# Moving bank-emptying copies and additions ahead of roundings, and the attention-row loads forward, at the start of a Strassen-style feed-forward

## The chip, the cores and the metric

The kernel runs on one core of a Trainium2 chip. The metric is device microseconds for one execution, as the median over runs. The other seven cores are not used.

## The reference, cut to what matters

Everything is float32; S = 2048 rows, D = 576 columns, H = 32 heads of 18, F = 4608.

```python
g = sigmoid((x * gate_w).sum(-1, keepdims=True))
# A: linear attention with a learned feature map (a pair of softmaxes per head)
phi_q, phi_k = softmax pairs of (q @ w_phi), (k @ w_phi)
a = (phi_q @ (phi_k^T v)) / (phi_q @ sum(phi_k) + 1e-6) @ wo
# B: gated ReLU feed-forward on the same x
b = (relu(x @ W_gate) * (x @ W_up)) @ W_down
out = g * a + (1 - g) * b
```

## The kernel before, in words

The kernel first computes the attention half (A) and writes its result, transposed and already scaled by the gate, to a DRAM tile `att` of 576 x 2048. Then it computes the feed-forward half (B), adding its results to rows of `att` that have been loaded back into SBUF, and writes the sums out.

All matrix products keep float32 accuracy by splitting each operand in a rounded high part and a low part ("high" is a copy on ScalarE into fp32r, "low" a subtraction on VectorE), and by multiplying high x high, high x low and low x high.

**The end of the attention half.** The 2048 columns are treated in four blocks of 512, in the order 3, 0, 1, 2 (`BLOCKS`), numbered b = 0 to 3. `project_out(b, m)` makes row block m of the output of block b: 14 matmuls for m < 4 and 9 for m = 4 into one PSUM bank, then `rows_out` copies the bank to SBUF on ScalarE (L796, or L798 and an addition on VectorE L799 for m = 4) and stores it to `att` (for b > 1 from GpSimd's queue). Its weights stand in four SBUF tiles of the pool `raw` (`WOUT`); the last projection, `project_out(3, 4)`, still reads three of them.

Between these last projections stands the preparation of the feed-forward. Seven sums of blocks of x, the operands of a seven-product (Strassen-Winograd) scheme, are numbered by their place in `SEQ = (1, 5, 6, 2, 7, 3, 4)`. Operands 3 to 6 are loaded in place: `high_in_place(0, i)` rounds one on ScalarE (L856, L857), `low_of_place(i)` makes its low part on VectorE (L861, L841), and `in_place(i)` does both. The weights of a unit are loaded to `wr` by `load_w`, rounded by `blocks`/`block_sums` with `high_w` (ScalarE L874), given low parts by `low_w` and `low_w_rows` (VectorE L877, L880), and their sums are formed by `sums_of_blocks` (VectorE L895 to L898). The results are `WB[u]` (tile `wb`) and `WS[u]` (tile `ws`), each in a pool of two buffers: those of unit u + 2 take the place of those of unit u. Because the second half of the rows needs the same weights again, the finished `wb` and `ws` are stored to DRAM (`wbd`, `wsd`), and a buffer is free for the next unit only when its store has landed.

**The units of the feed-forward.** There are 72 units u; each covers 128 columns of F for half of the rows. `step(u, j)`, j = 0 to 6, first issues one product of seven matmuls in the order of `SEQ`, then work on the other engines, then from the second pair of units on the down-projection of an earlier pair. The seven products use few banks, and accumulate on values that must first have been taken out:

- j = 0, product 1: a new bank `cx` (two in turn); j = 1, product 5: a new bank `ca` (one).
- j = 2, product 6: on top of `cx`, once `g1` has been copied from it (ScalarE L1299, issued at j = 1).
- j = 3, product 2: a new bank `cy`. j = 4, product 7: on top of `cx`, once `g2` has been copied (issued at j = 3).
- j = 5, product 3: on top of `ca`, once `u2` has been copied (issued at j = 2).
- j = 6, product 4: on top of `cx`, once `u2` has been added to it (VectorE L1420, issued at j = 5).

After that `g2` is added from `ca` (L1423) and gated (L1295), the last `cx` is gated at the next unit's j = 0, and the gated tiles are split (`hh` on ScalarE L1238, `hl` on VectorE L1243). Also in these steps: at j = 0 and 1 of unit u >= 1 the blocks of unit u + 1 are rounded and given low parts, at j = 2 their sums are formed, at j = 3 the sums are rounded, at j = 4 they get their low parts. At unit 0, j = 3 and 4, the down weights are rounded and given low parts (`plain_down`, L1096 and L1099).

**Order.** In this part the order on TensorE, VectorE, ScalarE, GpSimd and the SyncE queue (SP) is the order in which the code issues (`in_order`). So what stands behind a waiting instruction of the same engine waits too, and a DMA of SP behind one that waits. The attention rows of the first half are loaded by `load_acc` (L1141, eight times 256 KB) and `load_rest` (L1146, twice 128 KB) into `sums_of`, the four `raw` buffers that `WOUT` stood in.

Of the kernel before, what the change touches and what calls it, by code (L numbers as in the profile page):

```python
# [7 lines left out]
F32 = mybir.dt.float32  # L8
# [11 lines left out]
NC = F // P  # L20
# [63 lines left out]
def gated_mix_kernel(  # L84
# [717 lines left out]
    def project_out(b, m):  # L802

        i = 5 * (b - 1) + m + 1
        i = i % 2 if b < 3 else i % 4
        ps = pv1.tile([P, TB], F32, name="pw", tag="pv1") if i == 0 else kv_bank((2, 0, 1)[i - 1])
        accumulate(ps, [a for k in range(4, -1, -1) for a in pairs_of(b, m, k)])
        rows_out(b, m, ps)
# [135 lines left out]
    def in_place(i):  # L944
        high_in_place(0, i)
        low_of_place(i)

    def low_of_place(i):
        low_in_place(0, i)
        low_rest(0, i, tt)  # L950
# [48 lines left out]
    with in_order(tc, nc, nc.tensor, nc.vector, nc.scalar, nc.gpsimd, nc.sync):  # L999
        project_out(2, 1)  # L1000
        for k in (2, 1, 0):
            quotient(3, k)
        for k in (2, 1, 0):
            operand_rows(3, k)
        whole(x1)
        RS.close()
        pad = ctx.enter_context(tc.tile_pool(name="pad2", bufs=1, **R_))
        pad.tile([P, 24], F32, name="pad2")
        xo2 = ctx.enter_context(tc.tile_pool(name="xo2", bufs=4, **R_))
        wop = ctx.enter_context(tc.tile_pool(name="wop", bufs=2, **R_))  # L1010
        wraw = ctx.enter_context(tc.tile_pool(name="wraw", bufs=2, **R_))
        load_w(0)
        load_w(1)
        for i in range(3, 7):
            load_in_place(0, i)
        load_rests(0, (3, 4, 5))
        load_down(0)
        project_out(2, 2)
        blocks(0, high_w)
        low_parts(blocks, 0)  # L1020
        project_out(2, 3)
        project_out(2, 4)
        blocks(1, high_w)
        sums_of_blocks(0)
        operand_high(0, 2)
        project_out(3, 0)
        block_sums(0, high_w)
        low_parts(blocks, 1)
        operand_low(0, 2)
        load_rests(0, (6,))  # L1030
        load_w(2)
        low_parts(block_sums, 0)
        high_in_place(0, 3)
        project_out(3, 1)
        low_of_place(3)
        sums_of_blocks(1)
        high_in_place(0, 4)
        project_out(3, 2)
        block_sums(1, high_w)
        low_of_place(4)  # L1040
        high_in_place(0, 5)
        project_out(3, 3)
        low_parts(block_sums, 1)
        low_of_place(5)
        in_place(6)
        project_out(3, 4)
    AP.close()
    BS.close()
# [278 lines left out]
    def step(u, j):  # L1327


        g, odd = divmod(u, 2)  # L1330
        v, q = u + 1, g - 1
        plain, was_plain = g < NG or g == 2 * NG - 1, q < NG
        ps, first = bank(SEQ[j])
        product(ps, u, SEQ[j], first)
        add_up()
        make = 0 < u < NC - 1
        cx, ca, cy = (BANKS.get(n) for n in ("cx", "ca", "cy"))
        old = not odd and g > 0

        if j == 0:  # L1340
            if u > 0:
                last_cx, a = LATE.pop()
                gated(a, last_cx)
            if odd:
                EVEN[g] = LATE.pop(), a
            elif old:
                ODD[q] = EVEN.pop(q) + (LATE.pop(), a)
        e2, e1, o2, o1 = ODD[q] if old else EVEN[g] + (None, None) if odd else [None] * 4
        if odd and plain or old and was_plain:
            key, x2, x1 = ((g, 0), e2, e1) if odd else ((q, 1), o2, o1)  # L1350
            if j == 0:
                high_h(key + (1,), x2)
            elif j == 1:
                high_h(key + (0,), x1)
                low_h(key + (1,), x2)
            elif j == 2:
                low_h(key + (0,), x1)
        elif odd:
            if j == 1:
                high_h((g, 1), e1)  # L1360
            elif j == 3:
                low_h((g, 1), e1)
                minus(e2, e1)
            elif j == 4:
                high_h((g, 5), e1)
            elif j == 5:
                low_h((g, 5), e1)
        elif old:
            if j == 0:
                high_h((q, 6), e1)  # L1370
                minus(o2, e2)
            elif j == 1:
                high_h((q, 3), o2)
                low_h((q, 6), e1)
            elif j == 2:
                low_h((q, 3), o2)
                high_h((q, 7), e2)
                high_h((q, 2), o1)
            elif j == 3:
                minus(o1, e1)  # L1380
                low_h((q, 7), e2)
            elif j == 4:
                high_h((q, 4), e1)
                low_h((q, 2), o1)
            elif j == 5:
                low_h((q, 4), e1)

        if make:
            if j == 0:
                blocks(v, high_w)  # L1390
                if v + 1 < NC:
                    load_w(v + 1)
            elif j == 1:
                blocks(v, low_w)
                blocks(v, low_w_rows)
            elif j == 2:
                if v < NC - 2:
                    nc.sync.dma_start(wbd[v], WB.pop(v).bitcast(F32))
                sums_of_blocks(v)
            elif j == 4:  # L1400
                block_sums(v, low_w)
                block_sums(v, low_w_rows)
            elif j == 5:
                if v < NC - 2:
                    nc.sync.dma_start(wsd[v], WS.pop(v).bitcast(F32))
        elif j == 0 and NC < u < 2 * NC - 1:
            load_operands(v)

        if j == 1:
            T["g1"] = copy(cx, "g1")  # L1410
        elif j == 2:
            T["u2"] = copy(ca, "u2")
        elif j == 3:
            T["g2"] = copy(cx, "g2")
            if make:
                block_sums(v, high_w)
        elif j == 4:
            tt(out=T["g1"], in0=cy, in1=T["g1"], op=ADD)
        elif j == 5:
            tt(out=T["u2"], in0=cx, in1=T["u2"], op=ADD)  # L1420
        elif j == 6:
            a = T["g2"]
            tt(out=a, in0=ca, in1=a, op=ADD)  # L1423
            gated(a, T["u2"])
            if odd and not plain:
                minus(a, e1)
            LATE[:] = [a, (cx, T["g1"])]
            w = WO.pop(u)
            if NC - 2 <= u < NC:
                WO[u + 2] = w  # L1430

        if odd and plain and g > 0:
            if j == 2:
                plain_down(g, high)
            elif j == 3:
                plain_down(g, low)
        elif odd and not plain:
            prepare_down(g, 0, j)
        elif old and not was_plain:
            prepare_down(q, 1, j)  # L1440
        if old and j == 5:
            load_down(g)
        if old and j == 6:
            ODD.pop(q)
        if g > 0:
            s = 7 * odd + j
            PEND.append(down_plain(q, s) if was_plain else down(q, s, one_bank))

        swap_in(u, j)
        if u == 0:  # L1450
            if 3 <= j < 5:
                plain_down(0, (high, low)[j - 3])
            elif j == 5:
                nc.sync.dma_start(wbd[u], WB.pop(u).bitcast(F32))
                nc.sync.dma_start(wsd[u], WS.pop(u).bitcast(F32))
        if u == 1 and j < 2:
            (nc.sync.dma_start(wbd[u], WB.pop(u).bitcast(F32)) if j == 0 else
             nc.sync.dma_start(wsd[u], WS.pop(u).bitcast(F32)))
        if u == 1 and j == 6:
            for i in range(8):  # L1460
                load_acc(0, i // 2 % 2, i // 4, i % 2)
            load_rest(0)
        if u in (NC + 1, 2 * NC - 1) and j < 4:
            if j % 2 == 0:
                rest_copy(j // 2)
            else:
                rest_rows(u // NC - (u == NC + 1), j // 2)
        if u == NC + 1:
            if j == 6:
                store_rest(0, 0)  # L1470
                store_rest(0, 1)
                load_rest(1)
        if j == 6 and u < NC:
            if u >= 4:
                next(later_half, None)
            if u == NC - 3:
                for _ in later_half:
                    pass
                load_operand(1, 0)
                load_operand(1, 1)  # L1480
# [157 lines left out]
```

## Time and profile before

| what | value |
|---|---|
| median of 3 runs | 1583.54 us (1583.13 to 1584.26) |
| the profiled execution | 1582.98 us |
| its span | 1581.2 us (1.8 us lie around it) |
| TensorE busy | 1567.2 us, 99% |
| VectorE busy | 1189.2 us, 75% |
| ScalarE busy | 558.6 us, 35% |
| granted TensorE clock | 1.000 |
| DMA | 283.38 MB, mean 179 GB/s |

Times in the trace are microseconds from the start of the span. A row of the timeline gives the start, the duration, the engine, the line and operation, output<-input, how many instructions were merged, and in square brackets how long the engine had been idle before it and what ended that. Rows of an engine may overlap slightly, since the next instruction starts before the last one has drained. Unit 0 of the feed-forward begins at 338.30 us, unit 2 at about 364 us; the rest of the span is the other 70 units and the end.

### The profile page before, as it was taken

Reading aid. Unit: us, or ns where it says so; the run is one execution under the profiler, and the core shown is the slowest. Engines: PE = TensorE matmul, PEld = TensorE weight load, DVE = VectorE, ACT = ScalarE, POOL = GpSimd, SP = SyncE. Lnnn points to the kernel's source line nnn. Section 1 sums busy time; section 2 is a strip of 40 time slices with the busy share of each in tenths; the row PEclk is TensorE's granted clock in tenths of the full one; section 3 lists DMA queues with packets and bytes.
Section 4 is the critical chain, followed back from the end, with each engine's and each line's share of the span. In section 5 each row is a group of like instructions: output and inputs, shape, how many; then the busy total and the mean of one; then the engine's idle time right before and its main releaser. Section 6 shows DMA issues by size and latency. Waiting matters only on the chain.

```text
span 1581.2 us, 20182 instructions
## 1 busy us (share of the span) xinstructions
PE 1567.2 (99%) x7823; PEld 1311.4 (83%) x7823; DVE 1189.2 (75%) x1865; ACT 558.6 (35%) x918; POOL 175.1 (11%) x243
## 2 busy tenths in 40 slices
PE   9999999999999999999999999999999999999998
PEld 9999995677888888888888888888888888888887
DVE  4997775597787877887777777777767777777777
ACT  4344335563333333333333334232232322232321
POOL 0126521110000000000000002111111111111110
PEclk9999999999999999999999999999999999999999
DMA  5365315597755575556545516543443443543432
GB/s 172 108 214 185 146 50 158 168 350 253 256 201 212 212 278 204 201 212 224 196 172 206 220 44 236 191 183 132 153 183 132 162 160 131 178 159 132 185 136 75
DMA packets 64539, 283.38 MB, mean 179 GB/s; under 512 B 6802, under 2 KB 17298, under 8 KB 55740
## 3 DMA queue, kind: packets, MB, share of 16 engines
q1 hardware_dynamic: 61228, 270.34, 47.1%
q0 software_dynamic: 2352, 10.11, 1.9%
q10 hardware_dynamic: 864, 1.65, 0.3%
q8 instruction: 61, 1.00, 0.3%
q14 instruction: 34, 0.28, 0.1%
HBM read 172.07 MB, written 108.60 MB: 178 GB/s over the span
## 4 chain that ended last, share of the span: by engine, by line
PE 95%; DVE 3%; ACT 1%; DMA 0%; issue 0%; POOL 0%; SPq 0%; ACTq 0%; POOLq 0%
PE cx L1133 28%; PE ca L1133 14%; PE pd L1173 12%; PE pd L1196 10%; PE cy L1133 7%; PE kv L175 4%; PE pk L175 3%; PE pq L175 3%; PE pm L1173 2%; PE pm L1196 2%; PE kv L421 1%; PE po L562 1%; PE pv L237 1%; PE ptr L379 1%; PE pw L175 1%; PE psf L259 1%
## 5 line engine op out<-in xcount | busy, mean ns | idle before, releaser
L1238 ACT ACTIVATE hh<-g 128x512 fp32r<-128x512 f32 x195 | 120.0, 624 | 457.3 <-DVE g L1295 287.9
L1211 DVE TENSOR_TENSOR ac<-pd,ac 128x512 f32<-128x512 f32 x238 | 163.9, 689 | 144.4 <-PE pd L1196 144.2
L1133 PE MATMUL cx<-xo,ws 128*128 128x512 f32 x1008 | 252.0, 389 | 1.6 <-ACT g L1299 1.6
L1133 PE MATMUL ca<-xo,ws 128*128 128x512 f32 x1008 | 251.9, 389 | 0.0
L1133 PE MATMUL cx<-xo,wb 128*128 128x512 f32 x1008 | 249.0, 389 | 1.5 <-DVE u L1420 1.5
L1133 PEld LDWEIGHTS cx<-xo,ws 128*128 128x128 f32 x1008 | 189.2, 188 | 41.2 <-ACT g L1299 2.1
L1133 PEld LDWEIGHTS cx<-xo,wb 128*128 128x128 f32 x1008 | 188.2, 188 | 42.4 <-DVE u L1420 1.9
L1133 PEld LDWEIGHTS ca<-xo,ws 128*128 128x128 f32 x1008 | 189.2, 188 | 39.3
L1173 PE MATMUL pd<-hh,wd 128*128 128x512 f32 x576 | 200.7, 389 | 0.0
L1196 PE MATMUL pd<-hh,wd 128*128 128x512 f32 x476 | 185.2, 389 | 0.0
L1179 DVE TENSOR_TENSOR ac<-pd,ac 128x512 f32<-128x512 f32 x144 | 99.0, 688 | 105.6 <-PE pd L1173 102.8
L1243 DVE TENSOR_TENSOR hl<-g,hh 128x512 fp32r<-128x512 f32 x195 | 135.4, 694 | 1.9 <-ACT hh L1238 0.2
L1299 ACT ACTIVATE g<-cx 128x512 f32<-128x512 f32 x144 | 85.0, 590 | 129.2 <-PE cx L1133 129.1
L1173 PEld LDWEIGHTS pd<-hh,wd 128*128 128x128 f32 x576 | 108.1, 188 | 22.5
L1133 PE MATMUL cy<-xo,wb 128*128 128x512 f32 x504 | 125.9, 389 | 0.0
L1096 ACT ACTIVATE wd<-wdr 128x384 fp32r<-128x384 f32 (+1 forms) x106 | 62.3, 606 | 143.2 <-DMA wdr<-wd 143.2
L1173 PE MATMUL pd<-hl,wd 128*128 128x512 f32 x288 | 112.0, 389 | 0.0
L1133 PEld LDWEIGHTS cy<-xo,wb 128*128 128x128 f32 x504 | 94.6, 188 | 19.6
L1196 PEld LDWEIGHTS pd<-hh,wd 128*128 128x128 f32 x476 | 89.4, 188 | 18.5
L1196 PE MATMUL pd<-hl,wd 128*128 128x512 f32 x238 | 92.6, 389 | 0.0
L841 POOL TENSOR_TENSOR xo<-xr,xo 32x512 fp32r<-32x512 f32 x5 | 8.3, 1670 | 614.7 <-PE ca L1133 608.5
L874 ACT ACTIVATE ws<-wr 128x1536 fp32r<-128x1536 f32 x36 | 53.7, 1491 | 48.2 <-DVE wr L898 46.0
(256 smaller groups left out, 2572.1 us busy)
## 6 DMA issues: line engine op xcount, KB each, us to landing
wsd<-ws SPq DMA_DIRECT2D x34, 1280.0 KB
ws<-wsd SPq DMA_DIRECT2D x34, 1280.0 KB
wbd<-wb SPq DMA_DIRECT2D x34, 960.0 KB
wb<-wbd SPq DMA_DIRECT2D x34, 960.0 KB
wr<-wgu SPq DMA_DIRECT2D x36, 768.0 KB
wdr<-wd SPq DMA_DIRECT2D x36, 576.0 KB
eT<-et SPq DMA_DIRECT2D x10, 594.0 KB
xt<-xb SPq DMA_DIRECT2D x7, 768.0 KB
```

The lines of the kernel that those rows point to most:

```text
L175: nc.tensor.matmul(ps, w, m, start=i == 0, stop=i == len(pairs) - 1)
L237: nc.tensor.matmul(pv[i][c], m, w_[:, k, cs], start=k == 0 and n == 0, stop=k == 4 and n == 1)
L874: nc.scalar.activation(o[:, :, 0:3], a, AF.Copy)
L1096: nc.scalar.activation(o[:, 0], a, AF.Copy)
L1133: nc.tensor.matmul(ps, w, v, start=first and m == 0, stop=m == len(pairs) - 1, skip_group_check=True)
L1173: nc.tensor.matmul(ps, w, v, start=k == 0 and (i < 2 or first), stop=k == len(mms) - 1 and (i < 2 or last), skip_group_check=True)
L1179: tt(out=a, in0=ps, in1=a, op=ADD)
L1196: mm = lambda ps, w, v, a, z: nc.tensor.matmul(ps, w, v, start=a, stop=z, skip_group_check=True)
L1211: tt(out=a, in0=ps, in1=a, op=ADD)
L1238: nc.scalar.activation(h, src, AF.Copy)
L1243: tt(out=l, in0=src, in1=h.bitcast(F32), op=SUB)
L1299: nc.scalar.activation(a, ps, AF.Copy)
```

## The change

Three things change.

1. Among the last projections, the rounding of operand 5 (`high_in_place(0, 5)`) goes ahead of `project_out(3, 3)`, `block_sums(1, high_w)` goes behind it, and `in_place(6)` goes from ahead of `project_out(3, 4)` to unit 0, j = 1, behind the copy of `g1`.
2. In unit 1 the low parts of the block sums of unit 2 (`low_w`, `low_w_rows`) go from j = 4, ahead of the additions to `g1` and `u2`, to j = 5, behind them; the store of `ws` of unit 2 follows them as before.
3. The ten loads of attention rows go from the end of unit 1 to j = 0 of unit 0. On SP they now stand ahead of the stores of `wb` and `ws` of units 0 and 1 and of `load_w(3)`.

```diff
         high_in_place(0, 4)
         project_out(3, 2)
+        high_in_place(0, 5)
+        low_of_place(4)
+        project_out(3, 3)
         block_sums(1, high_w)
-        low_of_place(4)
-        high_in_place(0, 5)
-        project_out(3, 3)
         low_parts(block_sums, 1)
         low_of_place(5)
-        in_place(6)
         project_out(3, 4)
...
             elif j == 4:
-                block_sums(v, low_w)
-                block_sums(v, low_w_rows)
+                if u > 1:
+                    block_sums(v, low_w)
+                    block_sums(v, low_w_rows)
             elif j == 5:
-                if v < NC - 2:
+                if 2 < v < NC - 2:
                     nc.sync.dma_start(wsd[v], WS.pop(v).bitcast(F32))
...
         elif j == 5:
             tt(out=T["u2"], in0=cx, in1=T["u2"], op=ADD)
+            if u == 1:
+                block_sums(v, low_w)
+                block_sums(v, low_w_rows)
+                nc.sync.dma_start(wsd[v], WS.pop(v).bitcast(F32))
...
         if u == 0:
+            if j == 0:
+                for i in range(8):
+                    load_acc(0, i // 2 % 2, i // 4, i % 2)
+                load_rest(0)
+            elif j == 1:
+                in_place(6)
             if 3 <= j < 5:
                 plain_down(0, (high, low)[j - 3])
...
-        if u == 1 and j == 6:
-            for i in range(8):
-                load_acc(0, i // 2 % 2, i // 4, i % 2)
-            load_rest(0)
```

## The prediction

> **What bounds the kernel now.** The page comes first: it says which engine has no time to spare.
>
> ```profile
> span 1581.2 us, 20182 instructions
> PE 1567.2 (99%) x7823; PEld 1311.4 (83%) x7823; DVE 1189.2 (75%) x1865; ACT 558.6 (35%) x918; POOL 175.1 (11%) x243
> ```
>
> TensorE works for 1567.2 of 1581.2 us, so the change can only gain what TensorE stands idle. Next the waits of TensorE, longest first: only two of them lie where the change is made.
>
> ```profile
> PE cx L1133 <- ACT g L1299: 1.6, 1, 1.6
> PE cx L1133 <- DVE u L1420: 1.5, 1, 1.5
> ```
>
> Each occurred once. The timeline of TensorE shows where, and what each costs.
>
> ```profile
> 338.30 1.75 PE L1133 MATMUL cx<-xo,wb 128*128 128x512 f32 x7
> 339.89 1.75 PE L1133 MATMUL ca<-xo,ws 128*128 128x512 f32 x7
> ...
> 343.28 1.89 PE L1133 MATMUL cx<-xo,ws 128*128 128x512 f32 x7 [1.64 <-ACT g L1299]
> ...
> 359.28 1.75 PE L1133 MATMUL ca<-xo,ws 128*128 128x512 f32 x7
> 362.53 3.49 PE L1133 MATMUL cx<-xo,wb 128*128 128x512 f32 x14 [1.50 <-DVE u L1420]
> ```
>
> A product of seven matmuls occupies 339.89 - 338.30 = 1.59 us. Product 6 of unit 0 was therefore due at 341.48 and began at 343.28: 1.80 us lost, and its seven matmuls lasted 1.89 instead of 1.75, the matmuls right after a gap being slower: 0.14 more. Product 4 of unit 1 was due at 360.87 and began at 362.53: 1.66, and I take the same 0.14 for it. Together 1.94 + 1.80 = 3.74 us, 0.24% of the time. That is the most that the change can gain. 0.2% (3.17 us) is about what a measurement of this kernel can tell from no change, so the answer hangs on what is left of these 3.74.
>
> **The first stall.** ScalarE's timeline shows why the copy of `g1` came late:
>
> ```profile
> 337.08 1.49 ACT L874 ACTIVATE ws<-wr 128x1536 fp32r<-128x1536 f32 x1 [3.14 <-DVE wr L898]
> 338.48 1.04 ACT L856 ACTIVATE xo<-xo 128x1024 fp32r<-128x1024 f32 x1
> ...
> 339.94 0.58 ACT L796 ACTIVATE o<-kv 128x512 f32<-128x512 f32 x1
> 340.42 1.04 ACT L856 ACTIVATE xo<-xo 128x1024 fp32r<-128x1024 f32 x1
> ...
> 342.01 0.59 ACT L798 ACTIVATE o<-kv 64x512 f32<-64x512 f32 x1
> 342.63 0.60 ACT L1299 ACTIVATE g<-cx 128x512 f32<-128x512 f32 x1
> ```
>
> ScalarE idled 3.14 us for VectorE's sums, then ran the rounding of `ws`, operand 5, a bank copy, operand 6 and another bank copy, and only then `g1`, ready since 338.30 + 1.75 = 340.05. After the change operand 5 (338.48 to 339.94, 1.5 us) goes into the 3.14 us of idle time, which has room for it and for the bank copy (0.6) behind it. `ws` still starts at 337.08, the last bank copy follows at 338.5, and ScalarE is free at 339.1. `g1` is then copied at 340.1 to 340.7, before product 6 is due at 341.48. Operand 6 follows until 342.1; it delays `u2` to 342.7 and `g2`, whose product ends at 343.2, not at all. The first stall goes.
>
> **What is late next in unit 0: VectorE.**
>
> ```profile
> 336.97 1.22 DVE L861 TENSOR_TENSOR xo<-xo 128x1024 fp32r<-128x1024 f32 x1
> ...
> 342.85 1.23 DVE L861 TENSOR_TENSOR xo<-xo 128x1024 fp32r<-128x1024 f32 x1
> ...
> 344.82 0.68 DVE L799 TENSOR_TENSOR o<-o,kv 64x512 f32<-64x512 f32 x1
> 346.86 0.69 DVE L1418 TENSOR_TENSOR g<-cy,g 128x512 f32<-128x512 f32 x1 [1.36 <-PE cy L1133]
> 347.47 1.42 DVE L1099 TENSOR_TENSOR wd<-wdr,wd 128x1024 fp32r<-128x1024 f32 x2
> 348.80 0.68 DVE L1420 TENSOR_TENSOR u<-cx,u 128x512 f32<-128x512 f32 x1
> ```
>
> From 336.97 VectorE has no gap until L799 has run; the same work stands there after the change, in another order, so it is done at 344.82 + 0.71 = 345.53. Then come the addition to `g1`, the low part of the down weights and the addition to `u2`, which before followed each other at 0.61 and 1.33 us: 345.53, 346.14, 347.47, done at 348.15. Product 4 of unit 0 is due at 341.48 + 4 x 1.59 = 347.83. It waits for `u2` until 348.19: a new stall of 0.36 + 0.14 = 0.50 us. Before, TensorE's delay of 1.94 us covered this. Of the first stall 1.94 - 0.50 = 1.44 us are gained.
>
> **The second stall.** Low parts stood ahead of the additions:
>
> ```profile
> 357.72 1.49 ACT L874 ACTIVATE ws<-wr 128x1536 fp32r<-128x1536 f32 x1 [0.81 <-DVE wr L898]
> ...
> 359.24 1.22 DVE L877 TENSOR_TENSOR ws<-wr,ws 128x1024 fp32r<-128x1024 f32 x1 [1.61 <-ACT ws L874]
> 360.48 0.68 DVE L880 TENSOR_TENSOR ws<-wr,ws 32x512 fp32r<-32x512 f32 x1
> 361.19 0.69 DVE L1418 TENSOR_TENSOR g<-cy,g 128x512 f32<-128x512 f32 x1
> 361.80 0.68 DVE L1420 TENSOR_TENSOR u<-cx,u 128x512 f32<-128x512 f32 x1
> ```
>
> VectorE waited for ScalarE's rounding and then spent 361.19 - 359.24 = 1.95 us on L877 and L880 before it came to `g1` and `u2`. Moved behind `u2`, they no longer stand before product 4. Unit 1 begins at 348.19 + 1.59 + 0.14 = 349.92, its product 7 begins at 356.27 and ends at 358.0; `u2` is then added by 358.7, product 4 is due at 349.92 + 6 x 1.59 = 359.46. The stall goes, 1.80 us. The price: the low parts now stand before the addition of `g2` from `ca` and its gating. They end at 358.7 + 1.95 = 360.6, `g2` is out of `ca` at 361.3 and gated at 362.0 (0.7 us each, as the rows of L1418 and L1420); product 5 of unit 2 wants `ca` at 359.46 + 2 x 1.59 = 362.64. Cover 1.3 us; without it, up to 1.95 us would come back. What waits behind on ScalarE is the rounding of the gated tile, then `wb` of unit 3, then unit 2's `g1`, at about 364.9; before product 6 of unit 2 one down product (six matmuls, 1.36) is inserted, so it is due at 365.6. Cost nothing.
>
> **The loads on SP.** Here the queues change most.
>
> ```profile
> 332.78 0.33 SPq L870 DMA_DIRECT2D wr<-wgu  x1
> 333.16 0.43 SPq L1454 DMA_DIRECT2D wbd<-wb  x1
> ...
> 361.64 5.70 SPq L1141 DMA_DIRECT2D ac<-att  x8
> ```
>
> Before, the store of `wb` of unit 0 was issued at 333.16, and that of `ws` behind it. After, the ten loads stand ahead of them, and these wait for the `raw` buffers of the projection weights. One comes free as `project_out(3, 3)` ends, the others in the course of `project_out(3, 4)`: its nine matmuls of 1.59 / 7 = 0.23 us end just behind 338.30, so they began at 336.3, and with the 0.1 to 0.2 that a matmul takes to end the buffers come free between 336.4 and 338.5. So the stores come some ten us later, and ScalarE's rounding of `wb` of unit 2 may write only when the store of `wb` of unit 0 has landed:
>
> ```profile
> 351.95 1.15 ACT L874 ACTIVATE wb<-wr 128x1152 fp32r<-128x1152 f32 x1
> L1238 ACT ACTIVATE hh<-g 128x512 fp32r<-128x512 f32 x195 | 120.0, 624 | 457.3 <-DVE g L1295 287.9
> ```
>
> Behind it on ScalarE stand one `hh` (0.62) and unit 1's copy of `g1` (0.60). That copy is wanted by product 6 of unit 1, at 349.92 + 2 x 1.59 = 353.10. So the rounding must begin by 353.10 - 1.15 - 0.62 - 0.60 = 350.7; otherwise it can begin at 350.1, when product 4 of unit 0 is done with the buffer. When does the store land? The rates, from the windows; the last column is GB/s:
>
> ```profile
> 338.00:340.00 2.00, 2.00 (x11) 1.65 (x10) 1.94 (x3) 2.00 (x4) 0.00 (x0) 1.00 1.02 429
> ...
> 362.00:364.00 2.00, 1.47 (x6) 1.24 (x7) 1.77 (x3) 0.16 (x1) 0.00 (x0) 1.00 0.99 410
> 364.00:366.00 2.00, 2.00 (x10) 1.64 (x9) 1.54 (x3) 2.00 (x3) 0.00 (x0) 1.00 1.09 252
> 366.00:368.00 2.00, 2.00 (x11) 1.65 (x10) 1.18 (x2) 1.01 (x3) 0.00 (x0) 1.00 0.82 267
> 368.00:370.00 2.00, 2.00 (x11) 1.65 (x10) 0.16 (x1) 0.25 (x1) 0.00 (x0) 1.00 1.06 335
> 370.00:372.00 2.00, 2.00 (x11) 1.65 (x10) 1.97 (x4) 0.60 (x1) 0.00 (x0) 1.00 1.03 385
> ...
> 369.84 0.69 DVE L1179 TENSOR_TENSOR ac<-pd,ac 128x512 f32<-128x512 f32 x1 [2.65 <-DMA ac<-att]
> ```
>
> The store of a `ws` (1.31 MB) and the ten loads (2.36 MB) shared 362 to 372 us, the loads at 267 to 385 GB/s once the store was through: 6.1 to 8.8 us for the ten. By 368.0 some 2 x (0.410 + 0.252 + 0.267) = 1.86 MB had moved, the `ws` and two loads; the addition that needs the second load began at 369.84: 1.8 us from data moved to landed. After the change I let the loads' data move from 338.0, between the first and the last release (`load_w(2)`, issued at 332.78, goes first), with one `att` store among them (0.26 MB, 0.6 us): until 344.7 to 347.4. The `wb` store, 0.98 MB at 429 GB/s, takes 2.3 and 1.8 to land: 348.8 to 351.5, the middle 350.2. So its cost lies between nothing and 351.5 - 350.7 + 0.14 = 0.9 us. I take nothing, as the middle lies before 350.7. What follows on SP has more room. By the same rate `ws` of unit 0 lands 3.1 us behind it, at 353.3, and is wanted when `ws` of unit 2 is rounded, at 357.72 before and up to 1.9 earlier now; `load_w(3)` (0.79 MB) and `wb` of unit 1 land at 355.1 and 357.4 and are wanted at about 362.5, in unit 2's first step; `ws` of unit 1 lands at 360.5 and is wanted some steps later. The store of `ws` of unit 2, moved behind the additions, is wanted only two units on.
>
> The Trainium skill, "DMA: Bandwidth & Descriptors", section "Bandwidth", speaks against loads of this size: its table gives 138 GB/s at 64 KB and 341 at 1 MB and asks for 1 MiB per DMA; at some 250 GB/s for 256 KB, an estimate from that table, the ten would last 9.4 us, the store would land at about 352.1, and the gain would shrink to about 1.7 us. This trace agrees only in the first windows (252 and 267 GB/s); the later ones reach 385, as the loads queue up behind each other.
>
> VectorE's wait of 2.65 us for the loads in unit 2 (that last row) goes as well. That gains nothing, as TensorE waits for nothing there.
>
> **Sum.** 1.44 + 1.80 = 3.24 us. The profiled execution took 1582.98 us, 1.78 around its span, 0.56 below the median of the runs. It should become 1579.7 with a span of 1578.0, and the median 1583.54 - 3.24 = 1580.3.
>
> **The rivals.**
>
> *The store of `wb` is late (0.18).* For it: the loads' slow first windows, and transfers that were spread over 30 us now stand in one queue. Against: the middle of the estimate. A store landing between 350.7 and 352.5 takes 0.2 to 1.9 us back: 1580.5 to 1582.2, within 0.2%.
>
> *VectorE gets to `u2` in time (0.14).* If its chain is 0.4 us shorter than I add it up, the new stall in unit 0 vanishes and the gain is the whole 3.74: 1579.8. Against it: VectorE is packed without a gap from 336.97, and nothing of its work is taken away.
>
> *Slower (0.06): the loads wait for the last attention row.* `att` is one DRAM tile. If the loads are held until all of it is stored, not only the rows of blocks 0 and 1 that they read, they wait for the store behind L799:
>
> ```profile
> DMA to landing us min/median/max: 4.7/6.5/8.9
> ```
>
> L799 would end at 343.5, its store be issued at 344.1 and land, at the median of 6.5, at 350.6. From first issue to the landing of `wb` my estimate above takes 350.2 - 336.4 = 13.8 us, some 1.6 of it waiting for `load_w(2)`: the store lands at 362.8, and ScalarE is 12 us late for 350.7. That is 12 - 3.2 = 9 us slower, 1592.5. The tipping point is a landing at 350.7 + 3.2 = 353.9. Against it: the rows read are written by the projections of b = 1 and 2, well before. Such a stall would also be the only one here long enough for the clock. By the Trainium skill, "TensorE: Matmul & The Clock Gate", section "What's actually happening", an idle window of some 3.4 us halves the clock until a busy one has passed, which would add an estimated 1.7 us; no run here shows it.
>
> **How the numbers follow.** My forecast has 0.62. Its 3.24 us lie just above 3.17, and its terms are good to some 0.3 us, so I put 0.40 of it above 0.2% and 0.22 within. With the 0.14 of the full gain that makes faster 0.54, with the 0.18 of the late store same 0.40; slower is the last rival, 0.06. The forecast and the full gain, with runs that scatter by half a microsecond, reach from 1579.2; the late store reaches to 1582.2. The range 1579.2 to 1582.4 leaves out the slower case and the edges.
>
> **What would show it.** Right: TensorE's waits for `g` L1299 and for `u` L1420 at unit 1 are gone; a wait of some 0.4 us for `u` L1420 stands at about 348 us; unit 2 starts at about 361.1 instead of 364.3; SP issues the loads at 336 to 342 us; no wait of ScalarE for a DMA before `wb`. Wrong: an ACT `wb` L874 that idles for `wbd` at 350 to 352 us and a TensorE wait for `g` behind it, loads issued only after 350 us, or a stall in unit 2 for `g2` or `hh`.

## The result, and the profile after

| | median | lowest to highest | runs |
|---|---|---|---|
| before | 1583.60 us | 1582.97 to 1585.32 | 20 |
| after | 1581.57 us | 1580.04 to 1584.27 | 20 |

The ratio is 0.9986 [0.9980, 0.9992], 0.14% faster, and the medians lie 2.0 us apart. That is clear of the noise, but within the 0.2% that the prediction calls no change. The runs of after scatter over 4.2 us where those of before scatter over 2.4. The ratios here and below leave out the one slow run of all, 1736.76 us at a mean granted clock of 0.851, in experiment 8. The profiled execution of after happens to be the longest of its twenty, with 1584.27 us and a span of 1581.7, so its span shows no gain at all; the shortest span of the twenty is 1578.1, next to the 1578.0 that was forecast. Part of what separates them is seen below.

The page, and TensorE's waits (waiting instruction, releaser: us in total, times, longest), of the profiled execution of after:

```profile
span 1581.7 us, 20179 instructions
PE 1568.9 (99%) x7823; PEld 1312.1 (83%) x7823; DVE 1189.8 (75%) x1865; ACT 558.3 (35%) x918; POOL 175.2 (11%) x243
...
PE cx L1132 <- ACT g L1298: 1.9, 1, 1.9
```

Lines moved by one: the product's line 1133 is 1132 now, the copies' 1299 is 1298. Of the two old waits the one for VectorE's `u` is gone from the list. A wait for the copy `g` is still there, once and a little longer, but TensorE's timeline shows that it is another one:

```profile
338.33 1.75 PE L1132 MATMUL cx<-xo,wb 128*128 128x512 f32 x7
...
341.50 1.75 PE L1132 MATMUL cx<-xo,ws 128*128 128x512 f32 x7
...
346.26 1.75 PE L1132 MATMUL ca<-xo,ws 128*128 128x512 f32 x7
348.12 3.48 PE L1132 MATMUL cx<-xo,wb 128*128 128x512 f32 x14
...
355.07 2.54 PE L1132 MATMUL cx<-xo,ws 128*128 128x512 f32 x7 [1.89 <-ACT g L1298]
357.41 2.75 PE L1132 MATMUL cy<-xo,wb 128*128 128x512 f32 x7
360.00 1.75 PE L1132 MATMUL cx<-xo,ws 128*128 128x512 f32 x7
...
363.17 3.33 PE L1132 MATMUL cx<-xo,wb 128*128 128x512 f32 x14
```

Product 6 of unit 0 starts at 341.50, 3.17 us behind product 1, with no wait: the first stall is gone. Product 4 of unit 1 (363.17, the first half of 14 matmuls) starts with no wait: the second is gone too. The new stall is at product 6 of unit 1: 1.89 us idle, and then two products that take 2.54 and 2.75 us instead of 1.75. Why it waited, ScalarE's timeline tells:

```profile
340.11 0.60 ACT L1298 ACTIVATE g<-cx 128x512 f32<-128x512 f32 x1 [0.89 <-PE cx L1132]
...
349.50 0.63 ACT L1237 ACTIVATE hh<-g 128x512 fp32r<-128x512 f32 x1 [4.47 <-DVE g L1294]
352.85 1.16 ACT L874 ACTIVATE wb<-wr 128x1152 fp32r<-128x1152 f32 x1 [2.72 <-DMA wbd<-wb]
353.92 0.61 ACT L1237 ACTIVATE hh<-g 128x512 fp32r<-128x512 f32 x1
354.44 0.58 ACT L1298 ACTIVATE g<-cx 128x512 f32<-128x512 f32 x1
```

The rounding of `wb` of unit 2 could have started at 350.13 and waited 2.72 us until the store of `wb` of unit 0 had landed. The copy of `g1` stands behind it, two instructions on, and so started at 354.44. The SP queue and the windows show the store's way (last three columns of a window: granted clock, DMA share, GB/s):

```profile
336.48 4.61 SPq L1140 DMA_DIRECT2D ac<-att  x8
341.56 1.23 SPq L1145 DMA_DIRECT2D ac<-att  x2
343.16 0.45 SPq L1464 DMA_DIRECT2D wbd<-wb  x1
...
336.00:338.00 2.00, 2.00 (x10) 1.65 (x10) 1.97 (x3) 1.47 (x2) 0.46 (x1) 1.00 0.72 267
338.00:340.00 2.00, 2.00 (x11) 1.65 (x10) 1.94 (x3) 1.20 (x2) 0.07 (x1) 1.00 0.67 136
340.00:342.00 2.00, 2.00 (x11) 1.65 (x10) 1.95 (x3) 1.89 (x3) 0.00 (x0) 1.00 0.91 291
342.00:344.00 2.00, 2.00 (x11) 1.65 (x10) 1.94 (x4) 1.38 (x4) 0.04 (x1) 1.00 1.05 306
344.00:346.00 2.00, 2.00 (x10) 1.69 (x9) 1.94 (x3) 1.03 (x2) 0.52 (x1) 1.00 0.98 327
```

The ten loads are issued from 336.48, as forecast, and the store behind them at 343.16. While the loads are issued and run, 136 to 327 GB/s move. The store lands 9.7 us after its issue.

The two long products behind the gap are the clock. In the windows of one us the granted clock is 0.55, 0.50, 0.50 and 0.74 between 356 and 360, and 1.00 around that:

```profile
356.00:357.00 1.00, 1.00 (x5) 0.75 (x4) 0.97 (x3) 0.00 (x0) 0.00 (x0) 0.55 1.04 437
357.00:358.00 1.00, 1.00 (x4) 0.81 (x3) 0.93 (x3) 0.35 (x1) 0.00 (x0) 0.50 0.99 417
358.00:359.00 1.00, 1.00 (x4) 0.81 (x3) 0.54 (x1) 0.62 (x2) 0.00 (x0) 0.50 1.08 456
359.00:360.00 1.00, 1.00 (x5) 0.73 (x5) 0.00 (x0) 1.00 (x1) 0.00 (x0) 0.74 0.98 415
```

### The profile page after: what moved, and what is told of

It is laid out like the page before. It is cut to its first block, busy times and chain, and to the rows that moved or that the text cites. A ratio compares the mean times of both kernels' runs of the same rounds, so it can differ in the third digit from the quotient of the medians.

```text
span 1581.7 us, 20179 instructions
## 1 busy us (share of the span) xinstructions
PE 1568.9 (99%) x7823; PEld 1312.1 (83%) x7823; DVE 1189.8 (75%) x1865; ACT 558.3 (35%) x918; POOL 175.2 (11%) x243
## 3 DMA queue, kind: packets, MB, share of 16 engines
q10 hardware_dynamic: 864, 1.65, 0.3%
## 4 chain that ended last, share of the span: by engine, by line
PE 95%; DVE 2%; DMA 1%; ACT 0%; issue 0%; POOL 0%; SPq 0%; DVEq 0%; ACTq 0%; POOLq 0%
PE cx L1132 28%; PE ca L1132 14%; PE pd L1172 12%; PE pd L1195 10%; PE cy L1132 7%; PE kv L175 4%; PE pk L175 3%; PE pq L175 3%; PE pm L1172 2%; PE pm L1195 2%; PE kv L421 1%; PE po L562 1%; PE pv L237 1%; PE ptr L379 1%; PE pw L175 1%; PE psf L259 1%
```

## The experiments

**The measure.** The start of unit 0 itself lies between 338.3 and 341.5 us in the profiled executions of all kernels, two executions of after among them with 338.33 and 341.47: the attention half before it scatters by some 3 us, and this blurs totals. So beside the ratios I use the distance from product 1 of unit 0 to product 1 of unit 3 in TensorE's timeline. The places of unit 0 to 2 that the change touches lie within it. Most kernels, before among them, have one profiled execution and so one distance; the one kernel that was profiled twice without a late store repeats it to the hundredth (40.79). A stall found there costs more than the idle time listed: the idle time counts from the end of the last matmul, 0.16 us after the next one was due, and the product behind a gap takes 0.14 more. So a listed wait w costs w + 0.30, which gives the prediction's 1.94 and 1.80 for 1.64 and 1.50.

| kernel | unit 0 | unit 3 | distance | against before |
|---|---|---|---|---|
| before | 338.30 | 382.64 | 44.34 | |
| after, first profile | 338.33 | 383.12 | 44.79 | +0.45 |
| after, three more | 341.47, 338.32, 339.00 | 383.19, 380.63, 381.15 | 41.72, 42.31, 42.15 | -2.62, -2.03, -2.19 |
| loads back | 338.43 | 380.86 | 42.43 | -1.91 |
| stores first | 338.83 | 379.82 | 40.99 | -3.35 |
| copy first | 339.97 | 381.17 | 41.20 | -3.14 |
| loads only | 340.52 | 385.06 | 44.54 | +0.20 |
| part 1 only | 340.58 | 383.08 | 42.50 | -1.84 |
| part 2 only | 339.25 | 384.20 | 44.95 | +0.61 |
| stores first, copy first, low part last, two profiles | 338.99, 338.79 | 379.78, 379.58 | 40.79, 40.79 | -3.55, -3.55 |
| store later | 338.42 | 384.24 | 45.82 | +1.48 |

**The theories.** *The queue*: the store of `wb` lands late because it stands behind the ten loads on SP, and ScalarE, in order, carries the delay to `g1`. *The order on ScalarE*: the loads have little to do with it, the rounding ahead of `g1` in unit 1 is what is too much. Further theories belong to single experiments.

**1. The ten loads back in their old place, all else as in after.**

```diff
-            if j == 0:
-                for i in range(8):
-                    load_acc(0, i // 2 % 2, i // 4, i % 2)
-                load_rest(0)
-            elif j == 1:
+            if j == 1:
                 in_place(6)
...
+        if u == 1 and j == 6:
+            for i in range(8):
+                load_acc(0, i // 2 % 2, i // 4, i % 2)
+            load_rest(0)
```

> The changed kernel, but with the ten loads of attention rows back at the end of unit 1; the two reorderings stay. Queue theory (the loads ahead on SP hold up the store of wb of unit 0, and ScalarE's rounding of wb waits for it in front of unit 1's copy of g1): ScalarE's wait of 2.7 us for wbd and TensorE's of 1.9 us for g1 are gone, unit 2 begins at about 361.1, the time is 3.2 us below before, ratio 0.9980. Order theory (the reordering itself makes g1 late, by what it puts in front on ScalarE): the wait for g1 stays near 1.9 us and the ratio is that of the changed kernel, 0.9986.

Measured: 1581.97 us against 1583.57, ratio 0.9990 [0.9982, 0.9999]. The waits for the store and for `g1` are gone, as the queue theory has it, but the gain did not rise. VectorE now waits for the loads, and TensorE for VectorE:

```profile
369.25 0.69 DVE L1178 TENSOR_TENSOR ac<-pd,ac 128x512 f32<-128x512 f32 x1 [3.85 <-DMA ac<-att]
...
373.44 0.50 PE L1172 MATMUL pd<-hh,wd 128*128 128x512 f32 x1 [0.66 <-DVE ac L1178]
...
378.24 1.88 PE L1132 MATMUL cx<-xo,wb 128*128 128x512 f32 x7 [0.19 <-DVE u L1420]
```

By the distance, the two waits with what follows them, (0.66 + 0.27) + (0.19 + 0.30) = 1.42, are nearly all that is missing to the 3.35 of the next experiment (0.27: the first of six matmuls behind the gap started late and ran slower). Neither theory had counted on this: with the stalls gone, unit 2 comes so early that loads issued at the end of unit 1 are too late. The `g1` wait alone thus speaks for the queue theory here; its ratio of 0.9980 did not come.

**2. The stores of `wb` and `ws` of unit 0 ahead of the loads.**

```diff
             if j == 0:
+                nc.sync.dma_start(wbd[u], WB.pop(u).bitcast(F32))
+                nc.sync.dma_start(wsd[u], WS.pop(u).bitcast(F32))
                 for i in range(8):
                     load_acc(0, i // 2 % 2, i // 4, i % 2)
...
-            elif j == 5:
-                nc.sync.dma_start(wbd[u], WB.pop(u).bitcast(F32))
-                nc.sync.dma_start(wsd[u], WS.pop(u).bitcast(F32))
```

> The changed kernel, but with the stores of wb and ws of unit 0 issued ahead of the ten loads instead of behind them. Queue theory: the store lands about ten us earlier, ScalarE does not wait for it, TensorE's wait for g1 is gone, ratio 0.9980; the loads land some 5 us later than in the changed kernel, which nothing waits for. If instead the sheer number of bytes in this stretch is what delays ScalarE (volume theory), the wait moves to load_w(3) or to the store of wb of unit 1 and a stall of 1 us or more appears in unit 2: ratio 0.9985 or above. Order theory: 0.9986, wait for g1 unchanged.

Measured: 1580.34 us against 1583.57, ratio 0.9980 [0.9971, 0.9988], distance 3.35 shorter. ScalarE, SP and TensorE:

```profile
350.55 1.17 ACT L874 ACTIVATE wb<-wr 128x1152 fp32r<-128x1152 f32 x1
...
336.98 10.31 SPq L1140 DMA_DIRECT2D ac<-att  x8
...
348.63 3.47 PE L1132 MATMUL cx<-xo,wb 128*128 128x512 f32 x14
```

The rounding follows the `hh` ahead of it with no gap, TensorE waits neither for `g1` nor for the loads, though the eight of them now take 10.31 us to issue. No stall appears in unit 2 either, so the volume theory fails. The edit changes only the order on SP, and with it the wait is gone: the queue theory holds.

**3. In unit 1, the copy of `g1` ahead of the rounding and low parts of `wb`.**

```diff
             if j == 0:
-                blocks(v, high_w)
+                if u > 1:
+                    blocks(v, high_w)
...
-            elif j == 1:
+            elif j == 1 and u > 1:
                 blocks(v, low_w)
                 blocks(v, low_w_rows)
...
             T["g1"] = copy(cx, "g1")
+            if u == 1:
+                blocks(v, high_w)
+                blocks(v, low_w)
+                blocks(v, low_w_rows)
```

> The changed kernel, but in unit 1 the rounding of wb of unit 2, and its low parts, stand behind the copy of g1 on ScalarE instead of ahead of it. Queue theory: ScalarE still waits some 2.7 us for the store of wb, but with g1 already out of its bank; product 6 begins on time, unit 2 at about 361.1, ratio 0.9980 and a narrow spread of the runs. Volume theory: the copy of u2, now behind the waiting rounding, becomes the late one and TensorE waits about 1 us before product 3: ratio 0.9986.

Measured: 1580.62 us against 1583.57, ratio 0.9980 [0.9972, 0.9989], distance 3.14 shorter. ScalarE:

```profile
353.27 0.60 ACT L1298 ACTIVATE g<-cx 128x512 f32<-128x512 f32 x1 [0.23 <-PE cx L1132]
353.76 1.16 ACT L874 ACTIVATE wb<-wr 128x1152 fp32r<-128x1152 f32 x1
```

The wait of 2.7 us that was expected for the store doesn't appear: when the store lands isn't seen here, as the rounding comes to it later. But nothing that TensorE needs soon stands behind it any more. Both links of the chain are thus shown, each by cutting it alone: the late store (2) and the copy queued behind the rounding (3). What shows it is the wait that is gone and the distance, each in one profiled execution; by total time the intervals of 2 and 3 overlap with that of after.

**4. Only the loads moved (before, with the ten loads at unit 0, j = 0).** The question was whether the move costs something by itself.

```diff
+            if j == 0:
+                for i in range(8):
+                    load_acc(0, i // 2 % 2, i // 4, i % 2)
+                load_rest(0)
...
-        if u == 1 and j == 6:
-            for i in range(8):
-                load_acc(0, i // 2 % 2, i // 4, i % 2)
-            load_rest(0)
```

> The kernel before, with the ten loads moved to unit 0 and nothing else changed. Queue theory: the store of wb lands at about 352.9 again; with product 6 of unit 1 due at 354.5 here, g1 is late by about 0.5 us, and VectorE's chain behind the rounding by 0.9, so the second stall grows to about 1.9: 0.9 us slower than before, ratio 1.0006, more where the clock falls. Order theory: the move costs nothing, ratio 1.0000.

Measured: 1584.19 us against 1583.57, ratio 1.0004 [0.9994, 1.0013], distance 0.20 longer. This is inconclusive between the two expectations; ScalarE shows no wait for the store, since the old first stall delays all of unit 1. The second stall is still there, slightly longer than before:

```profile
364.94 3.51 PE L1133 MATMUL cx<-xo,wb 128*128 128x512 f32 x14 [1.64 <-DVE u L1420]
```

**5. Only the new order among the last projections (part 1).**

```diff
-        block_sums(1, high_w)
-        low_of_place(4)
         high_in_place(0, 5)
+        low_of_place(4)
         project_out(3, 3)
+        block_sums(1, high_w)
         low_parts(block_sums, 1)
         low_of_place(5)
-        in_place(6)
         project_out(3, 4)
...
         if u == 0:
+            if j == 1:
+                in_place(6)
```

> The kernel before with the first part of the change alone (operand 5's rounding ahead, operand 6 behind the copy of g1). Chain theory (in unit 1 the roundings and low parts form one chain that starts when the last step of unit 0 is done, so an earlier unit 0 also brings u2 of unit 1 earlier): the first stall goes, the second shrinks from 1.5 to about 1.2 us, unit 2 begins 1.8 us earlier after unit 0's start than before, ratio 0.9989. Additive theory, as the prediction had it: 1.44 us, the second stall unchanged at 1.5, ratio 0.9991.

Measured: 1581.92 us against 1583.53, ratio 0.9987 [0.9978, 0.9995], distance 1.84 shorter.

```profile
362.90 3.51 PE L1132 MATMUL cx<-xo,wb 128*128 128x512 f32 x14 [1.09 <-DVE u L1419]
```

The second stall shrank from 1.50 to 1.09 although its own cause was left in place. The terms are chained, not additive: the first stall gives 1.94 - 0.40 = 1.54 (product 4 of unit 0 starts 9.79 us behind product 1 instead of 6 x 1.59 = 9.54, and runs 0.15 slower), the second 0.41; together 1.95 against 1.84 measured. The ratio alone would not tell the two theories apart; the shorter wait does.

**6. Only the low parts behind `u2` (part 2).**

```diff
             elif j == 4:
-                block_sums(v, low_w)
-                block_sums(v, low_w_rows)
+                if u > 1:
+                    block_sums(v, low_w)
+                    block_sums(v, low_w_rows)
             elif j == 5:
-                if v < NC - 2:
+                if 2 < v < NC - 2:
                     nc.sync.dma_start(wsd[v], WS.pop(v).bitcast(F32))
...
             tt(out=T["u2"], in0=cx, in1=T["u2"], op=ADD)
+            if u == 1:
+                block_sums(v, low_w)
+                block_sums(v, low_w_rows)
+                nc.sync.dma_start(wsd[v], WS.pop(v).bitcast(F32))
```

> The kernel before with the second part alone (unit 1's low parts behind the addition to u2); the loads stay at the end of unit 1, now issued behind the later low parts. Additive theory: the second stall goes, 1.80 us, ratio 0.9989. Load theory (what the kernel with the loads put back showed: with VectorE's work moved back by the low parts, its wait for the second load delays an addition for which TensorE waits in unit 2): VectorE waits more than 3 us for the load, TensorE then waits some 0.7 to 1 us in unit 2, ratio 0.9994.

Measured: 1584.45 us against 1583.53, ratio 1.0004 [0.9996, 1.0013], distance 0.61 longer. The second stall is gone (1.80), and more than that is lost in unit 2. SP, VectorE's waits, TensorE:

```profile
363.50 5.69 SPq L1141 DMA_DIRECT2D ac<-att  x8
...
DVE ac L1179 <- DMA ac<-att: 4.8, 1, 4.8
...
376.76 0.50 PE L1173 MATMUL pd<-hh,wd 128*128 128x512 f32 x1 [1.63 <-DVE ac L1179]
...
381.55 1.89 PE L1133 MATMUL cx<-xo,wb 128*128 128x512 f32 x7 [0.19 <-DVE u L1421]
```

On SP the loads stand behind the store of `ws` of unit 2, which moved with the low parts: they are issued 24.25 us after unit 0 starts, where before it was 23.34, and unit 2 comes 1.8 us earlier. VectorE's wait for them grows from 2.65 to 4.8 and reaches TensorE: (1.63 + 0.27) + (0.19 + 0.30) = 2.39, and 2.39 - 1.80 = 0.59 of the measured 0.61. The load theory was right in kind, but had priced TensorE's wait at 0.7 to 1 us. This is what the third part of the change, the earlier loads, is needed for.

**7. Stores first, copy first, and the low part of the down weights behind `u2` in unit 0.** Experiments 2 and 3 together, and

```diff
-            if 3 <= j < 5:
-                plain_down(0, (high, low)[j - 3])
+            if j in (3, 5):
+                plain_down(0, high if j == 3 else low)
```

> The changed kernel with three more moves: the stores of wb and ws of unit 0 ahead of the loads, the rounding of wb in unit 1 behind the copy of g1, and in unit 0 the low part of the down weights behind the addition to u2. If the wait of 0.3 us in unit 0 for u2 is what is left, it goes as well, with the 0.14 behind it: from unit 0's start to the end 0.4 us less than in the kernel with the stores first, ratio 0.9977. If the low part of the down weights in its new place makes g2 or the gated tile late instead, the wait moves to unit 1 and the ratio stays 0.9980.

Measured: 1580.22 us against 1583.53, ratio 0.9973 [0.9964, 0.9983], distance 3.55 shorter.

```profile
348.51 3.34 PE L1132 MATMUL cx<-xo,wb 128*128 128x512 f32 x14
```

Product 4 of unit 0 starts 9.52 us behind product 1, on time, and its matmuls run at full pace: the last of the stalls, for `u2` in unit 0, is gone as well. Against experiment 3 that is 41.20 - 40.79 = 0.41 us, the 0.27 of the wait and the 0.14 behind it. Of the 3.74 us that the prediction called the most, 3.55 are reached. The missing 0.2 is the price of experiment 3, present there too: product 6 of unit 2 starts 0.08 us late and takes 1.88 to 1.89.

**8. The store still later: the load of the next weights (`load_w(3)`, 0.79 MB) ahead of it too.**

```diff
-                if v + 1 < NC:
+                if v + 1 < NC and u > 1:
                     load_w(v + 1)
...
                 load_rest(0)
+                load_w(3)
             elif j == 1:
                 in_place(6)
```

> The changed kernel with load_w(3), 0.79 MB, ahead of the store of wb of unit 0 as well, so that this store lands about 1.8 us later still. Queue theory: ScalarE's wait for it grows from 2.7 to about 4.5 us, TensorE's wait for g1 from 1.9 to about 3.7, and the clock falls to half behind it in every run: 2 us slower than the changed kernel, ratio 1.0000 to before. If the late store matters only in the rare run (the profile of the changed kernel was its slowest), the ratio stays at 0.9986 to 0.9990.

Measured: 1585.04 us against 1583.53, ratio 1.0007 [0.9999, 1.0016], distance 1.48 longer than before.

```profile
354.00 1.16 ACT L874 ACTIVATE wb<-wr 128x1152 fp32r<-128x1152 f32 x1 [3.77 <-DMA wbd<-wb]
...
356.22 3.04 PE L1132 MATMUL cx<-xo,ws 128*128 128x512 f32 x7 [2.95 <-ACT g L1298]
...
356.00:357.00 1.00, 0.78 (x3) 0.64 (x4) 0.95 (x3) 0.66 (x2) 0.00 (x0) 0.81 1.08 456
357.00:358.00 1.00, 1.00 (x4) 0.81 (x3) 0.96 (x3) 0.00 (x0) 0.00 (x0) 0.50 1.01 425
```

More bytes ahead of the store, a later landing (354.00 instead of 352.85 in the first profile of after), and the delay goes on one to one, 1.05 us on ScalarE and 1.06 on TensorE. That profile was after's latest, as the next runs show: against the other three, with 1.25 to 1.84 us on ScalarE, the wait grew by 1.9 to 2.5, where a landing 1.8 later was expected. The clock drops again.

**9, 10, 11. After itself three times more.** What was open: does the store land late in every execution, or is the profiled one an outlier? The kernel is unchanged.

> The changed kernel once more, unaltered. Always-late theory (the store of wb lands late in every execution, by a varying amount): ScalarE waits 1 to 3 us for it, TensorE 0.2 to 2 us for g1, the clock falls only where TensorE's wait is near 2 us; ratio 0.9986. Rare-late theory (the first profile was an exception): no wait for g1, product 1 of unit 3 begins 41.0 us after unit 0's start as in the kernel with the stores first; ratio near 0.9980.

> The changed kernel unaltered, another execution, for the spread. Always-late theory: again a wait of ScalarE for the store of wb of 1 to 3 us. Rare-late theory: none.

> The changed kernel unaltered, a further execution, for the spread. Always-late theory: again a wait of ScalarE for the store of wb of 1 to 3 us. Rare-late theory: none.

Measured, 9: 1581.05 us against 1584.45, ratio 0.9984 [0.9975, 0.9993]; 10 and 11, one execution each, 1581.82 and 1581.46. ScalarE and TensorE of the three, in this order:

```profile
354.52 1.17 ACT L874 ACTIVATE wb<-wr 128x1152 fp32r<-128x1152 f32 x1 [1.25 <-DMA wbd<-wb]
...
356.75 1.89 PE L1132 MATMUL cx<-xo,ws 128*128 128x512 f32 x7 [0.43 <-ACT g L1298]
```

```profile
351.97 1.17 ACT L874 ACTIVATE wb<-wr 128x1152 fp32r<-128x1152 f32 x1 [1.84 <-DMA wbd<-wb]
...
354.19 1.89 PE L1132 MATMUL cx<-xo,ws 128*128 128x512 f32 x7 [1.02 <-ACT g L1298]
```

```profile
352.50 1.17 ACT L874 ACTIVATE wb<-wr 128x1152 fp32r<-128x1152 f32 x1 [1.69 <-DMA wbd<-wb]
...
354.72 1.89 PE L1132 MATMUL cx<-xo,ws 128*128 128x512 f32 x7 [0.86 <-ACT g L1298]
```

The first profile included, the store is late in four of four, by 1.25 to 2.72 us on ScalarE: the always-late theory holds. TensorE loses 0.73, 1.32 and 1.16 us (wait + 0.30), and here product 6 takes 1.89, so the clock did not drop. These losses make up the distances: 41.72 - 40.99 = 0.73, 42.31 - 40.99 = 1.32, 42.15 - 40.99 = 1.16, each just the loss of its wait against stores first. For the first profile 44.79 - 40.99 = 3.80: 2.19 for its wait and 1.6 for the clock (from product 6 to product 4 of unit 1 it takes 363.17 - 355.07 = 8.10 us, in the execution of 10 it takes 6.50).

**12. The kernel of 7 once more, beside 9.**

> The kernel with the stores first, wb rounded behind g1 and the down weights' low part behind u2, once more, on the chip that times the changed kernel: no wait of TensorE from unit 0 to unit 3, 40.8 us from product 1 of unit 0 to that of unit 3; 1.2 to 2 us faster than the changed kernel if the late store is what that one loses, the same if it is not.

Measured: 1581.07 us against 1584.45, ratio 0.9978 [0.9968, 0.9988]; TensorE waits for nothing between unit 0 and unit 3, and the distance is 40.79 again. Against before its ratios say 0.27% and 0.22% faster in the two comparisons. Against after the 1.2 to 2 us that were expected do not show in the total time: the medians of 9 and 12 are 1581.05 and 1581.07, and the intervals of their ratios, 0.9984 and 0.9978, overlap. By the distance it is 0.9 to 1.5 us shorter than the three later profiles of after, and 4.0 shorter than the first. So the gain over after is shown in this stretch of the trace, and not in the totals.

## Why the prediction was right or wrong

**The median, 1580.3 with 1579.2 to 1582.4; measured 1581.57.** The range holds it. The forecast's likeliest case did not come true: the late store of `wb`, its first rival at 0.18 with 1580.5 to 1582.2, did, in every profile of after, and the median lies within its price. So the range held because it had been widened for a rival thought unlikely; the gain of over 0.2%, to which the prediction gave 0.54, was not reached.

**The first stall.** Right to hundredths: `g1` copied at 340.11 (forecast 340.1), product 6 at 341.50 (341.48).

**VectorE late in unit 0.** Right, in this row by row: `g1`, the down weights and `u2` at 345.44, 346.05 and 347.38, each 0.09 earlier than added up:

```profile
345.44 0.69 DVE L1418 TENSOR_TENSOR g<-cy,g 128x512 f32<-128x512 f32 x1
346.05 1.42 DVE L1098 TENSOR_TENSOR wd<-wdr,wd 128x1024 fp32r<-128x1024 f32 x2
347.38 0.69 DVE L1420 TENSOR_TENSOR u<-cx,u 128x512 f32<-128x512 f32 x1
```

Product 4 was due at 346.26 + 1.59 = 347.85 in this execution, by the start of product 3, and began at 348.12: 0.27 late where 0.36 was forecast, and 0.14 slower. So the rival in which VectorE comes in time did not occur. Experiment 7 takes this wait away and gains the 0.41.

**The second stall, and the low parts behind it.** The stall went. The cover of 1.3 us was there: `g2` is added at 364.41 and out of `ca` at 365.10, and product 5 of unit 2 starts at 366.35:

```profile
364.41 0.69 DVE L1427 TENSOR_TENSOR g<-ca,g 128x512 f32<-128x512 f32 x1
...
366.35 1.75 PE L1132 MATMUL ca<-xo,ws 128*128 128x512 f32 x7
```

**The sum, 3.24 us.** The right sum for the kernel without the late store: 3.35 in the distance and 1583.57 - 1580.34 = 3.23 in the medians of experiment 2. That the medians agree so closely is partly luck, as the interval of that ratio reaches from 0.12 to 0.29%. As the worth of each part by itself the two terms were wrong. The parts alone are worth 1.84 and -0.61, not 1.44 and 1.80, because a stall removed early moves the later ones (5) and brings unit 2 to its loads sooner (6).

**"The store lands between 348.8 and 351.5; I take nothing."** This is the step that failed. Counted from the start of unit 0 the estimate was 10.5 to 13.2 us, middle 11.9, deadline 12.4. Measured were 14.5, 13.05, 13.65 and 13.5: one at the late end of the range and three beyond it. The term was mis-sized by the choice of the middle. In the first profile 136 GB/s moved from 338 to 340, half of the 267 that was taken as the slow end. In the four profiles 255 to 309 GB/s moved, all transfers together, from the start of unit 0 to the issue of the store, which came only 4.6 to 5.3 us after that start. What the 7.8 to 9.7 us from the store's issue to its landing are made of the profile doesn't separate. The cost was 0.73 to 1.32 us in three profiles and 3.8 in one, where the estimate had at most 0.9. The 1.3 us by which the median missed the forecast are of the size of the three. The rival's own price ended at 1.9, as it had the wait alone and not the clock.

**"VectorE's wait for the loads gains nothing when it goes."** True only while TensorE's stalls delay unit 2. Once they are gone the wait is worth 1.4 us (1) or 2.4 (6).

**The late loads of the slower rival** didn't occur: the loads are issued from 336.48, SP waits only 0.4 us for an `att` store before one of them, and in no profile of after does VectorE wait for them.

**The clock.** The prediction put the drop only beside its slowest rival, as a stall long enough. It came already after 1.89 us. The Trainium skill, "TensorE: Matmul & The Clock Gate", section "What's actually happening", has half clock after at least one idle window of some 3.4 us and full clock after a busy one of that length, in windows that run freely. This case agrees with the half (0.50) and with the length of the slow stretch: (1 - 0.55)/0.5 + 1 + 1 + (1 - 0.74)/0.5 = 3.4 us below full clock. It doesn't agree that 3.4 us of idleness are needed: 1.89 were enough, and the measurement decides.

**By the estimate from the Trainium skill's table** the gain would have been about 1.7 us; the median's 2.0 lies nearer to that than to 3.24, and its landing of 352.1, 13.8 behind the start of unit 0, lies among the 13.05 to 14.5 measured. The Trainium skill, "DMA: Bandwidth & Descriptors", section "Bandwidth", gives the 138 GB/s at 64 KB and 341 at 1 MB in a table of loads issued from GpSimd, while the loads here are issued from SP. The estimate came out nearer to this case than the middle of the trace's rates did. That the size of the loads is the reason no run here shows, since the windows don't separate the loads from other transfers.

## What to carry to other kernels

When a batch of loads is moved ahead of a store on one queue, the store's landing is a new deadline: put the store first, or take everything urgent out from behind the instruction that needs the store's buffer. Each of the two alone took away the wait that the batch had brought (2 and 3). And where a term's estimate straddles its deadline, its price is not nothing: take the late end as seriously as the middle, and price the parts of a change in chain, since a wait that costs nothing now may be the next one to be reached.

## What the runs showed of the hardware

- TensorE's clock went to 0.50 after an idle time of 1.89 us and of 2.95 us, for 3.4 us, at a cost of some 1.6 us. It stayed at 1.00 after 0.43, 0.86 and 1.02 us, and after the waits of 1.63 to 1.65 in before, loads only and part 2 only. The drop began after TensorE was busy again, 1.0 us in after and 0.4 us in store later (0.81 in its window from 356, which is 0.38 us at half). Where the bound lies between 1.65 and 1.89, and whether it is one, wasn't tried.
- From 338 to 340 in the first profile of after, 136 GB/s moved while the DMA engines were busy for 0.67 of the time. The loads were still being issued, the eight of them from 336.48 to 341.09, so how much of this is the pace of their issue and how much the loads themselves isn't shown. In the same stretch of stores first, with the stores ahead, 421 to 441 GB/s moved:

```profile
338.00:339.00 1.00, 1.00 (x6) 0.84 (x5) 0.97 (x2) 1.00 (x1) 0.54 (x1) 1.00 1.05 441
339.00:340.00 1.00, 1.00 (x6) 0.80 (x6) 0.97 (x2) 0.69 (x2) 0.00 (x0) 1.00 1.00 421
```

- The start of the feed-forward, 338 us into the span, varies by some 3 us between executions of one kernel, more than the whole effect studied here.
